# A gated linear attention with an MLP behind it on one core: the first unit is given an order of its own

## The chip, the cores and the metric

The kernel runs on one core of one Trainium2 chip. A core has five engines with a queue of instructions each: TensorE (PE, matrix products, with its weight loads shown as PEld), VectorE (DVE), ScalarE (ACT), GpSimd (POOL) and SyncE (SP, which here only issues DMAs). The engines run side by side and wait for one another through semaphores. Products are written to PSUM, a small memory that the program divides into banks; everything else lies in SBUF. The metric is the time of one execution on the device in microseconds (us).

## The reference, cut to what matters

```python
batch, n_heads, seq, head_dim = (4, 8, 768, 48)

f = 1.0 / (1.0 + np.exp(-f_logit))
state = np.zeros((B, H, D, D), dtype=np.float32)
for t in range(S):
    state = f[:, :, t, :, None] * state + np.einsum('bhd,bhe->bhde', k[:, :, t], v[:, :, t])
    y[:, :, t] = np.einsum('bhd,bhde->bhe', q[:, :, t], state)

x = attn_out.transpose(0, 2, 1, 3).reshape(B * S, H * D)       # 3072 x 384
h = x @ w_in                                                   # 384 x 2048
g = h * (1.0 / (1.0 + np.exp(-1.702 * h)))
out = g @ w_out                                                # 2048 x 384
```

All arrays are float32. A state of 48 x 48 for each of 32 heads decays by a gate of its own in each of its 48 rows, takes up one outer product per token and is read by the query. The result, with heads joined, goes through an MLP with a quick gelu.

## The kernel before, in words

**Units.** The 3072 tokens are cut into twelve units of 256 tokens with all eight heads (`NALL` = 12, `U` = 256, L65 and L81). Each unit is done by `attention(n)`, and its output goes to the MLP as `xT`. Units 0 to 2 (`N_FILL` = 3) are done in one way, later ones in another that does not concern us. Within a unit, chunks of 64 tokens are the grain: inside a chunk the products of gates are built up in six levels (`LEV` = 1, 2, 4, ..., 32, `NL` = 6), between chunks a state is carried.

**What one of the first units does.** `load_raw` (L245) fetches the gate logits, q and k (called j = 0, 1, 2) into `raw`. `turn` (L334) transposes them on PE against an identity, two pieces of eight products each, and ACT copies each piece out of PSUM with two instructions; for the gates that copy is the sigmoid, in units 1 and 2 a tanh with POOL's `half_up` behind it. The three calls are `begin_f`, `begin` (for q) and `begin_k`; the last also sets aside `Kc` for level 0. `begin_gates` has POOL multiply the gates up, level by level, into `tot`.

A level (`level(l)`, L520) then does four things. `score` (L409) multiplies `Kc` of the level with the queries, sixteen products on PE, into a PSUM tile `sc` of two banks of which there is one. `promote` (L484) multiplies k and q by the gates of the level on DVE, an instruction for each, in place in `X`; it then lets ACT copy the next `Kc` (`set_aside`, L468). The q promotion follows the scores, as these read the queries. `evacuate` (L437) copies the scores under a mask into `A`: level 0 by a product with the mask, levels 1 to 4 by two `copy_predicated` on DVE, level 5 by four copies on ACT. The next level's scores write the same `sc`, so they wait for that copy.

Behind the levels come `turn_k` (L550), which turns k back through PE, and the part "S": `add` (L506) starts the values `y` from `A` and v, then the chunk products (L604) of `kn` with v go to PSUM and DVE forms the four states `st` from them, alternating a product with the gates (L622) and a sum (L623). Half of v is used in reversed order; `reverse_v` (L302) makes that with a `stream_shuffle` on DVE. The last part, "W", adds the states' share to `y` (L644), ACT copies `y` to `yT` (L656) and SP sends it to `xT`.

**The MLP and the weights.** Weights arrive as raw bits in pairs (`fetch_weights`, L192, three in flight), and each pair is converted by a Prelu on ACT (`begin_pair`, L208) and four DVE operations (L225 to L228), one for each call of `convert`. The products with w_in are L1034, those with w_out L1048.

**The order.** For units 0 to 3 the order in which instructions are emitted is the order of every engine's queue. `parts_of` lists a unit's parts and puts the next unit's `begin_...` between them; `merge` emits them, and between the parts a share of MLP work from `fill` and a number of converts. Unit 0 has no MLP work beside it; a list tells how many converts follow which part:

```python
fill = []
merge(0, fill, 0, steady, deal=(0, 0, 0, 0, 0, 0, 0, 3, 0, 0, 1, 2))
fill += mlp_blocks((0, 0)) + mlp_blocks((0, 1))
merge(1, fill, UNIT // 2 - LAG // 2 - 3 * DM, steady, 12, hold=1)
```

Here 12 stands for pairs' halves: 24 converts within unit 1. `keep_up` (L108) puts products on PE whose results nobody reads. PSUM tiles other than `sc` and `y` come from `bank` (L103), four lanes of one bank in turn.

Of the kernel before, what the change touches and what calls it, by code (L numbers as in the profile page):

```python
# [23 lines left out]
def kernel(  # L24
# [33 lines left out]
    nc = tc.nc  # L58
# [42 lines left out]
    turns = count()  # L101

    def bank(shape, name, lane=None):  # L103

        lane = next(turns) % 4 if lane is None else lane
        return ps.tile(shape, F32, tag=f"mm{lane}", name=name, bufs=1)
# [207 lines left out]
    def attention(n):  # L314
# [19 lines left out]
        def turn(j, outs, fn=None):  # L334
# [12 lines left out]
            for j0 in range(0, R, 4):  # L347
# [14 lines left out]
            if fn and n:  # L362
                half_up()
# [9 lines left out]
        def begin_f():  # L373
            def decay():
                turn(0, lambda f: F[:, ORDER.index(f) * SLOT:(ORDER.index(f) + 1) * SLOT], sigmoid)
# [5 lines left out]
            if n >= N_FILL or (n == 1 and 0 == 0):  # L381
                load_raw(n + 1, 0)
# [26 lines left out]
        def score(s, l, rhs):  # L409

            for a in range(NP):
                for h, g in TILES:
                    x = (a * NG + g) * HS
                    nc.tensor.matmul(  # L414
                        t["sc"][g * HS:(g + 1) * HS, h, a, s, :], lhsT=t["Kc", l][rows(h), x:x + HS], rhs=rhs(h, a, g),
# [17 lines left out]
        def scores():  # L433
            t["sc"] = ps.tile([P, 2, NP, 2, HS], F32, tag="sc", name=f"sc_{n}_{next(serial)}")
            return t["sc"]

        def evacuate(*levels):  # L437


            for s, l in enumerate(levels):  # L440
                m = LEV[l]
                if m == 1:
                    nc.vector.tensor_tensor(  # L443
                        view(A, 0, [[HALF, 2 * NP], [HS + 1, 2], [2, 32]]),
                        t["sc"].rearrange("p h a s (f t) -> p (h a) s f t", f=2)[:, :, s],
                        masks[:, l].unsqueeze(1).broadcast_to((P, 2 * NP, 2, 32)), ALU.mult,
                    )
                    continue
                if m == 32:

                    for p in range(0, P, 32):
                        f = 1 - p // 32 % 2
                        nc.scalar.copy(
                            view(A[p:p + 32], f * (HS + m), [[HALF, 2 * NP], [1, m]]),
                            t["sc"].rearrange("p h a s t -> p (h a) s t")[p:p + 32, :, s, f * m:(f + 1) * m],
                        )
                    continue
                for at, f in ((HS + m, 1), (0, 0)):
                    dims = [[HALF, 2 * NP], [2 * m, 32 // m], [1, m]]
# [823 lines left out]
```

## Time and profile before

| what | value |
|---|---|
| time, median of 3 runs (lowest to highest) | 609.05 us (609.04 to 609.99) |
| the profiled execution: its own time | 609.42 us |
| its span | 607.6 us |
| mean granted clock of PE | 0.992 |
| PE busy | 580.7 us (96%) |
| DVE busy | 435.0 us (72%) |
| ACT busy | 292.1 us (48%) |
| POOL busy | 139.6 us (23%) |
| chain that ended last | PE 70%, DVE 14%, ACT 6%, issue 4% |

The span is what the trace covers; the time also has what lies around it, 1.8 us in the profiled execution. All positions in the text (such as 14.65) are us from the span's start. The page cuts the span into 40 slices of 15.2 us and gives an engine's busy share of each in tenths; PEclk is the clock that PE was granted, in tenths of full speed. In the timeline a line has start, duration, engine, line of the program, operation, output <- inputs with shapes, the number of instructions, and in brackets the idle time before it with what ended that. The trace counts the products of the scores, turns and other float32 products twice: 32 for the sixteen of a level. "issue" is time in which an engine waited for nothing that the profile shows; SPq and ACTq are the DMA issues of these two engines.

### The profile page before, as it was taken

What the parts mean: (1) busy time and instruction counts of PE and PEld (TensorE: products, weight loads), DVE (VectorE), ACT (ScalarE), POOL (GpSimd) and SP (SyncE); (2) the same over time, 40 slices, a digit from 0 to 9 for tenths busy, and PEclk for the clock granted to TensorE, in tenths of its full rate; (3) what the DMA queues carried; (4) which work ended last, traced back from release to release, by engine and by line L of the source; (5) the groups of instructions that cost most, each with busy time, mean ns of one, the idle gap of its engine ahead of it and who ended that gap; (6) DMA issues with size and microseconds to landing.
All of it is one profiled execution on the core that took longest, in us unless ns stands there. A gap on an engine that the chain in (4) does not pass through costs nothing.

```text
span 607.6 us, 18486 instructions
## 1 busy us (share of the span) xinstructions
PE 580.7 (96%) x7824; PEld 516.5 (85%) x7824; DVE 435.0 (72%) x693; ACT 292.1 (48%) x611; POOL 139.6 (23%) x215
## 2 busy tenths in 40 slices
PE   6769899979999999999999999999999999999897
PEld 5657676847677689999999999999999999999897
DVE  1788976575894967788867888868778686462284
ACT  4475644433332444456465474575474563552440
POOL 3020020050032423240522312502502502303000
PEclk9988999989999999999999999999999999999999
DMA  6847766652034245245443243443352111001000
GB/s 173 209 107 187 176 163 172 140 140 79 1 96 101 77 126 130 50 114 132 92 127 90 68 129 97 118 125 69 93 143 63 55 54 30 27 3 26 28 1 27
DMA packets 83315, 58.30 MB, mean 96 GB/s; under 512 B 33633, under 2 KB 75265, under 8 KB 83233
## 3 DMA queue, kind: packets, MB, share of 16 engines
q1 hardware_dynamic: 82480, 55.94, 36.8%
q10 hardware_dynamic: 753, 1.18, 0.7%
q8 instruction: 62, 1.02, 0.7%
q14 instruction: 20, 0.16, 0.1%
HBM read 43.98 MB, written 8.39 MB: 86 GB/s over the span
## 4 chain that ended last, share of the span: by engine, by line
PE 70%; DVE 14%; ACT 6%; issue 4%; SPq 2%; POOL 2%; DMA 2%; DVEq 0%; ACTq 0%; POOLq 0%
PE h L940 15%; PE h L1034 10%; PE o_Y L803 9%; PE o L1048 7%; PE o_Z L803 6%; PE h_y L940 6%; PE sc L414 5%; PE o_W L803 3%; PE o_X L803 3%; PE t L352 2%; ACT yT L656 2%; POOL tot L405 2%; DVE g L968 1%; PE sc L604 1%; PE y L513 1%
## 5 line engine op out<-in xcount | busy, mean ns | idle before, releaser
L1034 PE MATMUL h<-xT,w_in 128*128 128x256 f32 x384 | 90.2, 390 | 1.2 <-DVE sum L1100 0.6
L473 ACT COPY Kc<-X 128x512 f32<-128x512 f32 x72 | 48.3, 671 | 81.4 <-DVE X L502 57.2
L1034 PEld LDWEIGHTS h<-xT,w_in 128*128 128x128 f32 x384 | 73.2, 194 | 14.0 <-DVE sum L1100 1.2
L502 DVE TENSOR_TENSOR X<-X,tot 128x1024 f32<-128x1024 f32 x45 | 57.4, 1275 | 33.9 <-PE sc L414 23.6
L1048 PE MATMUL o<-w_out,g 128*128 128x384 f32 x192 | 67.7, 502 | 2.7 <-DVE w_out L228 2.3
L1048 PEld LDWEIGHTS o<-w_out,g 128*128 128x128 f32 x192 | 36.2, 194 | 26.2 <-DVE w_out L228 2.9
L405 POOL TENSOR_TENSOR tot<-F 128x512 f32<-128x512 f32 x12 | 12.5, 1041 | 195.9 <-DVE st L622 189.6
L940 PE MATMUL h<-E,w_in 128*128 128x128 f32 (+1 forms) x420 | 53.4, 275 | 0.0
L803 PE MATMUL o_Y<-T,S 128*128 128x192 f32 x288 | 50.6, 329 | 0.0
L940 PEld LDWEIGHTS h<-E,w_in 128*128 128x128 f32 x420 | 50.1, 192 | 0.0
L1038 ACT ACTIVATE g<-h 128x256 f32<-128x256 f32 x64 | 24.0, 383 | 51.9 <-PE h L1034 51.5
L970 ACT ACTIVATE g<-g 128x512 f32<-128x512 f32 (+1 forms) x63 | 35.6, 585 | 25.6 <-DVE g L968 25.0
L803 PEld LDWEIGHTS o_Y<-T,S 128*128 128x128 f32 x288 | 46.8, 190 | 0.5
L656 ACT COPY yT<-y 48x256 f32<-48x256 f32 x96 | 35.2, 367 | 21.0 <-PE y L644 19.9
L464 DVE COPY_PREDICATED A<-masks,sc 128x256 f32<-128x256 uint32 x96 | 42.2, 509 | 0.0
L968 DVE TENSOR_TENSOR g<-g,h 128x512 f32<-128x512 f32 (+1 forms) x52 | 31.8, 632 | 12.7 <-PE h L940 11.5
L367 POOL TENSOR_SCALAR F<-F 128x1024 f32<-128x1024 f32 x11 | 15.1, 1369 | 112.0 <-ACT F L370 89.6
L414 PE MATMUL sc<-X,Kc 48*64 48x64 f32 x1440 | 31.1, 222 | 9.5 <-DVE A L443 3.5
L414 PEld LDWEIGHTS sc<-X,Kc 48*64 48x64 f32 x1440 | 26.3, 136 | 16.2 <-issue 8.3
L340 DVE STREAM_TRANSPOSE X<-raw 128x512 f32<-128x512 f32 x36 | 38.2, 1110 | 0.2
L902 POOL TENSOR_TENSOR E<-xT 128x128 f32<-128x128 f32 (+1 forms) x32 | 20.2, 643 | 75.3 <-DMA xT<-yT 34.7
L968 DVE TENSOR_TENSOR g<-g,h_y 128x512 f32<-128x512 f32 (+1 forms) x26 | 16.5, 633 | 21.8 <-PE h_y L940 18.3
(153 smaller groups left out, 1178.2 us busy)
## 6 DMA issues: line engine op xcount, KB each, us to landing
bits<-in_moe_w_out_dram SPq DMA_DIRECT2D x8, 768.0 KB, 5.5
raw<-in_f_logit_dram SPq DMA_DIRECT2D x48, 96.0 KB, 2.5
raw<-in_k_dram SPq DMA_DIRECT2D x48, 96.0 KB, 3.1
raw<-in_q_dram SPq DMA_DIRECT2D x44, 96.0 KB, 2.3
bits<-in_moe_w_in_dram SPq DMA_DIRECT2D x7, 576.0 KB, 5.2
k_tok<-z SPq DMA_DIRECT2D x56, 64.0 KB, 1.7
kt<-k_tok SPq DMA_DIRECT2D x14, 256.0 KB, 3.0
xT<-yT SPq DMA_DIRECT2D x24, 144.0 KB, 2.6
```

Of the source, the lines that this page charges most:

```text
L340: nc.vector.transpose(view(out, at, [[HALF, NP], [step, R4], [R4 * step, 32]]), by_half[:, j, f].rearrange("p a (j d) -> p (a j) d", j=R4) ...
L414: nc.tensor.matmul(t["sc"][g * HS:(g + 1) * HS, h, a, s, :], lhsT=t["Kc", l][rows(h), x:x + HS], rhs=rhs(h, a, g), start=True, stop=True,)
L464: moved = nc.vector.copy_predicated(out=view(A, at, dims), mask=mask.bitcast(U32), data=got)
L473: nc.scalar.copy(c.rearrange("p (n two m) -> p n two m", two=2, m=m), view(X, KF * SLOT, [[2 * m, SLOT // (2 * m)], [(KR - KF) * SLOT + m, ...
L502: nc.vector.tensor_tensor(x, x, y, ALU.mult)
L656: nc.scalar.copy(view(yT[rows(h)], at, [[U, NP], [step, HS]]), py[columns(h, g), g, :, f, :])
L803: nc.tensor.matmul(t[name], lhsT=lhs(f), rhs=rhs(f), start=(new and i == 0), stop=(i == HF - 1), skip_group_check=True,)
L940: nc.tensor.matmul(ph[:, t], lhsT=WA[a][:, f * P:(f + 1) * P], rhs=E[n][b], start=(root and t == 0), stop=not goes_on, skip_group_check=True,)
L968: nc.vector.tensor_tensor(to, to, part, ALU.add if sign > 0 else ALU.subtract)
L970: nc.scalar.activation(to, to, AF.Gelu_apprx_sigmoid)
L1034: nc.tensor.matmul(ph, lhsT=w_in[:, c, ff * P:(ff + 1) * P], rhs=xTs[n][:, c, :], start=(c == 0), stop=(c == NK - 1))
L1048: nc.tensor.matmul(t["po"], lhsT=g[ff // FG][:, ff % FG, tt * P:(tt + 1) * P], rhs=w_out[:, ff, :], start=(ff == ffs[0]), stop=(ff == ffs[ ...
```

## The change

The first unit leaves `merge` and gets a function of its own, `opening`, which emits its work in another order; later units keep theirs.

- The first weight pair is fetched by SP instead of ACT, behind f and k of unit 0. k is turned ahead of q; `begin_gates` comes ahead of both; the dummy products between the turns go.
- The loads of unit 1's k come ahead of v's, q's behind v's.
- Scores of levels 0 and 1 go to lanes 0 and 1 (`lane_scores`), of levels 2 and 3 to the tile `y`, of levels 4 and 5 to `sc`. `open_level` does scores and promotion only.
- Unit 1's f is turned in two halves, behind levels 2 and 3. One dummy product follows levels 0, 1 and 4, where two followed each of the levels 0 to 2 before.
- The masked copies (`open_evacuate`; here named `evacuate`) follow all levels, in the order 0, 5, 1, 2, shuffle of v, 3, 4. For levels 0 and 1 the tile is in two lanes, so that each copy is two instructions.
- The gelu's table is loaded by a gelu of four numbers ahead of `turn_k`.
- The chunk products come ahead of the values, into lanes 0 and 1; k of unit 1 is turned between them. A copy of one number of `y` onto itself stands on ACT behind the values.
- Four converts follow the states; 26 instead of 24 fall into unit 1.

```diff
     def bank(shape, name, lane=None):
-        lane = next(turns) % 4 if lane is None else lane
+        if lane is None:
+            lane = chosen.pop(0) if chosen else next(turns) % 4
         return ps.tile(shape, F32, tag=f"mm{lane}", name=name, bufs=1)
...
+        def lane_scores(*two):
+            t["sc"] = [bank([P, NP, 2, HS], f"sc_{n}_{next(serial)}", lane) for lane in two]
+            t["both"] = [(h * NP, x.rearrange("p a s t -> p a s t")) for h, x in enumerate(t["sc"])]
...
+        def open_level(l):
+            if l % 2 == 0:
+                lane_scores(0, 1) if l == 0 else scores("y" if l == 2 else "sc")
+            by_level[l] = t["both"]
+            score(l % 2, l, queries(l))
+            promote(l)
+
+        def open_evacuate(l):
+            for c, sc in by_level[l]:
+                evacuate_one(l, c, sc[:, :, l % 2])
...
         @part("S")
         def _():
-            add()
-            pd = scores().rearrange("p h a s t -> p h (a s t)")
+            if n:
+                add()
+                pd = scores().rearrange("p h a s t -> p h (a s t)")
+                pd = [pd[:, g] for g in range(NG)]
+            else:
+                pd = [bank([P, NP * 2 * D], f"pd_{g}", g) for g in range(NG)]
...
+            if not n:
+                units[1][0][2]()
+                add()
+
+                seen = t["py"][HS:HS + 1, 1, 0, 1, :1]
+                nc.scalar.copy(seen, seen)
             load_v(n + 1)
...
-    load_raw(0, 1, (nc.scalar,))
-    fetch_weights(nc.scalar)
-    begin_f, *begin = units[0][0]
-    begin_f()
-    keep_up(2)
-    for fn in begin:
-        fn()
-    load_raw(1, 0)
-    load_v(0)
-    load_raw(1, 1)
-    load_raw(1, 2)
-    fetch_weights()
-    fetch_weights()
+    def opening():
+        begin_f, begin, begin_k, begin_gates = units[0][0]
+        next_f, next_q, next_k, next_gates = units[1][0]
+        level, evacuate, turn_k = units[0][2]
+        load_raw(0, 0)
+        load_raw(0, 2)
+        load_raw(0, 1, (nc.scalar,))
+        fetch_weights()
+        begin_f()
+        begin_gates()
+        begin_k()
+        begin()
+        load_raw(1, 0)
+        load_raw(1, 2)
+        load_v(0)
+        load_raw(1, 1)
+        fetch_weights()
+        fetch_weights()
+        for l in range(NL):
+            chosen[:] = [2, 3][l % 2:][:1]
+            level(l)
+            if l in (2, 3):
+                next_f((0, 4)[l - 2:][:1])
+            elif l < NL - 1:
+                keep_up(1)
+            if l == 1:
+                begin_pair(0)
+                state["begin"] = 1
+
+        nc.scalar.activation(q_end, q_end, AF.Gelu_apprx_sigmoid)
+        chosen[:] = [2, 3]
+        turn_k(0)
+        turn_k(2)
+        evacuate(0)
+        evacuate(NL - 1)
+        for l in range(1, NL - 1):
+            evacuate(l)
+            if l == 2:
+                units[0][3]()
+        chosen[:] = [2, 3, 2, 3]
+        next_q()
+        units[0][1][-2][1]()
+        next_gates()
+        for _ in range(NOP):
+            convert()
+
     fill = []
-    merge(0, fill, 0, steady, deal=(0, 0, 0, 0, 0, 0, 0, 3, 0, 0, 1, 2))
+    opening()
     fill += mlp_blocks((0, 0)) + mlp_blocks((0, 1))
-    merge(1, fill, UNIT // 2 - LAG // 2 - 3 * DM, steady, 12, hold=1)
+    merge(1, fill, UNIT // 2 - LAG // 2 - 3 * DM, steady, 13, hold=1)
```

## The prediction

> **What bounds the kernel now.** I read the page's forty slices first, then the chain of waits, then the timeline of the first 85 us, where the change is.
>
> ```profile
> PE   6769899979999999999999999999999999999897
> DVE  1788976575894967788867888868778686462284
> PEclk9988999989999999999999999999999999999999
> ```
>
> The slices show PE at 90% or more from about 135 us to near the end; only the first slices have room. A change to the first unit must therefore hand an earlier start to a PE-bound remainder. In the opening three things hold PE back.
>
> ```profile
> 5.95 2.31 ACTq L205 DMA_DIRECT2D bits<-in_moe_w_in_dram  x2
> ...
> 8.31 1.21 ACT L357 ACTIVATE F<-t 128x256 f32<-128x256 f32 x4 [6.08 <-PE t L352]
> ...
> 19.67 0.69 PE L414 MATMUL sc<-X,Kc 48*64 48x64 f32 x32 [0.82 <-DVE A L464]
> 20.43 0.69 DVE L498 TENSOR_TENSOR X<-X,tot 128x512 f32<-128x512 f32 x1 [0.38 <-PE sc L414]
> 21.04 0.75 DVE L464 COPY_PREDICATED A<-masks,sc 128x256 f32<-128x256 uint32 x2
> 21.93 0.69 PE L414 MATMUL sc<-X,Kc 48*64 48x64 f32 x32 [0.29 <-DVE A L464]
> ...
> 29.14 0.69 PE L414 MATMUL sc<-X,Kc 48*64 48x64 f32 x29 [1.84 <-issue]
> ...
> 33.00 1.21 PE sc L604 x60
> ```
>
> (The last line is from the chain of waits, the others from the timeline.) First, ACT issues weight DMAs until 8.26 and so begins the sigmoid late. Second, a level's scores wait for the masked copy (L464) of the level before, because they share one PSUM buffer. Third, the states' products (L604) stand behind the values (L513) and the last copies.
>
> ```profile
> 34.43 0.35 DVE L619 COPY st<-sc 128x192 f32<-128x192 f32 x1
> ...
> 37.12 1.70 DVE L228 TENSOR_TENSOR w_in<-a,s 128x768 f32<-128x768 f32 x1
> ...
> 38.92 0.78 DVE L225 TENSOR_SCALAR s<-a 128x768 int32<-128x768 int32 x1
> ...
> 40.30 1.42 DVE L498 TENSOR_TENSOR X<-X,F 128x512 f32<-128x512 f32 x2
> ...
> 42.47 1.13 PE L414 MATMUL sc<-X,Kc 48*64 48x64 f32 x32 [3.29 <-DVE A L443]
> ...
> 43.85 5.23 PE L1034 MATMUL h<-xT,w_in 128*128 128x256 f32 x12 [0.25 <-DMA xT<-yT]
> ...
> 51.67 0.69 DVE L498 TENSOR_TENSOR X<-X,tot 128x512 f32<-128x512 f32 x1 [1.52 <-PE sc L414]
> ```
>
> This is the hand-over to unit 1, whose first promotion starts at 40.30. PE idles 3.29 us and comes back slow: 12 h products take 5.23 us, against 2.86 at 51.53. The clock by windows:
>
> ```profile
> 28.00:30.00 2.00, 0.86 (x31) 0.79 (x32) 0.13 (x1) 0.13 (x1) 0.00 (x0) 1.00 0.69 136
> ...
> 42.00:44.00 2.00, 1.28 (x33) 1.12 (x33) 1.97 (x3) 0.60 (x1) 0.00 (x0) 0.50 0.43 98
> ...
> 48.00:50.00 2.00, 2.00 (x22) 1.52 (x22) 1.97 (x3) 0.38 (x1) 0.00 (x0) 0.83 0.99 211
> 60.00:80.00 20.00, 17.86 (x364) 13.40 (x363) 19.09 (x32) 14.26 (x31) 4.67 (x6) 1.00 0.69 161
> 80.00:100.00 20.00, 20.00 (x168) 14.80 (x167) 13.47 (x25) 7.21 (x15) 0.07 (x1) 1.00 0.63 150
> ```
>
> After the window come the busy times of PE, PEld, DVE, ACT and POOL, the granted clock, the DMA share and GB/s. The clock is 0.50 until about 48.6. From 60 to 80 us DVE is full (19.09 of 20), from 80 to 100 PE is.
>
> **The change, part by part.** I follow the new instruction order with the old durations.
>
> *Start.* The 2.31 us of weight DMAs leave ACT's queue, and k is turned before q. The first sixteen f matmuls are half of 3.44 us (done at 6.4), the rest at 8.10; F is complete near 8.9 instead of 9.52. Without four dummies (8.04 to 9.31) k's turn follows at 8.11 and q's behind it, four pieces of 0.93 (64 in 3.71 us), done at 9.04, 9.97, 10.90, 11.83. ACT copies each piece in 0.66, with Kc 0 (0.84) between k and q: done 12.95. First scores at 13.0 instead of 14.65: 1.65 earlier. Weights now stand on SP ahead of the next f, at most 2.31 us, but that f waits for PE until 8.14 anyway. Unknown: whether q, used at 9.97, lands later beside weights issued 1 us sooner. Zero to 1 us; I take zero, as PE took q at 9.38 without a wait.
>
> *Levels.* With three bank pairs the wait on the copy goes. The next wait is the q promotion: scores to its start 0.76 (19.67 to 20.43), itself 0.69, then about 0.17 to the next scores: 1.62 a level, against 2.26 (19.67 to 21.93). The other path, k promotion (0.68), Kc copy (0.62) and two hops, is shorter. The Prelu put into ACT's order (0.93) and F's copies (0.66 each) fit beside it; unit 1's f pieces take 0.95 of PE's 0.92 gap. Its weights, issued by 7.2, land by 14.7 (longest row 7.5 us); the Prelu comes at 15.7. POOL's tot, now ending near 12.1, can stretch the first k promotion by 0.74 (L228 took 1.70 beside it and 0.96 alone); hidden, as the q promotion comes only at 13.8. Sixth scores: 13.0 + 5 x 1.62 = 21.1; last promotion ends at 22.55, before at 30.56. That includes the 1.84 us PE stall at 27.30, whose cause the trace doesn't show. I take it as gone from the path: the same number of PE instructions is now reached in q's turn for unit 1, where PE has slack. If it returns on the path, +1.84.
>
> *Copies behind.* Nothing hides them: DVE does level 0 (0.68), 1 (1.09 to the next start), 2 (0.68), the shuffle (0.49), 3 and 4 (0.68 each), 4.3 us, plus 0.2 for the split instructions and a short hop: shuffle done at 25.8, all at 27.15. v's second half lands by 21.1 (SP issued it until 15.44, now 1.79 later with k ahead of it, longest row of v 3.9), so 4 us of cover before the shuffle. Unit 1's q, behind both, lands at 23.1 by the longest row (issue until 17.33 + 1.79, then 4.0); its turn comes at 23 and PE has 1 us to spare before the states' products. ACT's gelu table load (1.28, was at 45.50) and four level 5 copies (1.51) end at 25.1.
>
> *States ahead.* Products need the shuffle: PE 25.95 to 27.15 (1.21), hiding behind the last copies. Seven state operations took 2.69 (34.43 to 37.12): done at 30.0, so 7.1 earlier. On PE the k turn (1.97) and values (1.11) end at 30.2; ACT's new 1x1 copy lies between zero and 0.20 (the 128x1 ACTIVATE at 2.02) plus two hops of 0.15; I take 0.5. State products 30.75 to 31.85, eight yT copies (3.02) to 34.97. Before, yT ended at 40.61 and h began 3.24 later: h now at 38.2, 5.65 earlier.
>
> *Hand-over.* Before, w_in, s and a took 3.18 us from 37.12 to 40.30. Now four converts stand there: 0.78 + 0.64 + 0.96 + 1.70 beside POOL's tot = 4.08. Unit 1's first promotion at about 34.15, 6.15 earlier; but two converts of pair 1 (1.4) are no longer done, so **4.75** of DVE work gained. (6 + 24 converts become 4 + 26: the later two fall into DVE's full stretch.) Later on SP, q_end's two DMAs (0.43 each) move ahead of weights; hidden, since SP waited 6.1 us there for DVE.
>
> *Clock.* sc_8 and its dummy end at 33.4; the next scores need the promotion and copy, 34.15 + 2.14 = 36.3. PE idles 2.9 us. Idle of 1.84 us (28 to 30) left the clock at 1.00; idle of 2.33 did not:
>
> ```profile
> 126.59 5.19 PE L1048 MATMUL o<-w_out,g 128*128 128x384 f32 x10 [2.33 <-DVE w_out L228]
> ...
> 128.00:129.00 1.00, 1.00 (x3) 0.59 (x2) 1.00 (x2) 0.00 (x0) 1.00 (x1) 0.50 1.02 390
> ```
>
> So I take half clock again, as before: h takes its 5.23, the scores at 50.91 come 5.65 earlier, q promotion at 46.0. One convert of 0.56 to 0.96 is outstanding there: 4.9, agreeing with 4.75. If the gap came out under 1.84 and the clock stayed, h would take 2.86, scores would come at 42.9, and DVE would set the pace: 34.15 + 9.17 (40.30 to 49.47) + 1.16 - 0.96 for the regrouped converts + 0.68 = 44.2, which is 1.8 more.
>
> The Trainium skill, page "TensorE: Matmul & The Clock Gate", section "Part 1: The HAM clock gate (the "warmup" mystery)", puts the fall to half rate after at least one idle window of about 3.4 us. By that rule 2.9 us idle would keep the clock and the gain would be 6.6, an estimate; the row with 2.33 us idle and a clock of 0.50 contradicts it.
>
> *Downstream.* The chain of waits from 51.7 to 75 is nearly all DVE, after 79.6 mostly PE, and DMA falls to a share of 0.00 at 150 to 160: nothing runs to a fixed clock. Bounds: none or all of the lead arrives. I take all.
>
> **Sum.** 4.8 off the profiled execution's 609.42 (span 607.6 and 1.8 around it) is 604.6. The median of three runs is 0.37 lower: **604.3**.
>
> **Rivals.**
> *Levels don't shorten.* If the Kc copy or promotion keeps the period at 2.26, 5 x 0.64 = 3.2 goes back: 607.5. For: ACT is in order and now holds Prelu and turns. Against: Kc 4 was ready at 23.09 and its scores waited for t pieces, not for it.
> *The lead is swallowed.* Later waits keep their places: 609, within 0.2%. For: PE also idles at 124 to 126 behind DVE. Against: those DVE operations are themselves relative.
> *Slower: the opening goes cold.* Four groups of dummies of 1.34 us become three of about 0.67. If PE falls to half clock at the 1.1 us gap before 13.0 and stays there, six scores cost 0.43 more each (1.13 against 0.70): 2.6; turns 1.5 for 32 (3.44 against 1.97), twice: 3.0; the products' 64-matmul groups of 1.1 about double, three times: 3.3. Less 4.8 that is +4: 613. It decides when more than half of that is met. Against: idle of 1.63 (13.02 to 14.65) and 1.84 kept the clock.
>
> **Chances and range.** Likeliest, 0.58 (its own range 601.8 to 606). Levels or the PE stall taking back part, 0.16. Swallowed, 0.09. Slower by cold clock or late loads, 0.17. Low end: 4.8 + 1.8 + 1.1 for two later DVE waits (0.84 at 54.6, 0.31 at 59.2) that an earlier PE would spare: 601.4, rounded to 601.5. High: the stall 1.84, q 1.0 and most of the levels' case: 608. 0.2% (1.2 us) is what measurement can tell: faster 0.74, same 0.09, slower 0.17.
>
> **What would show it.** First scores near 13.0; score spacing near 1.6 with no wait for a masked copy; states done near 30; unit 1's first promotion near 34; h at 38; the granted clock 0.50 after 36; PE solid from 75. Wrong if scores wait for ACT, if the clock is 0.50 before 30, or if SP's loads for unit 1 land after 23.

## The result: no change that can be measured

The changed kernel takes 609.51 us (median of 12 executions, 608.47 to 612.0), the kernel before 609.04 us (12 executions, 608.64 to 611.69): a ratio of 1.0003, 95% interval 0.9988 to 1.0017. (The ratios here and below are those on record with their intervals; they are not quotients of two medians.) The forecast of 604.3 was wrong. The profiled execution of the changed kernel took 609.87 us, with a span of 608.0 (before: 609.42 and 607.6) and a mean granted clock of 0.986 (before: 0.992).

From the page of the changed kernel, busy tenths in 40 slices of 15.2 us:

```profile
PE   7869899969999999999999999999999999999897
DVE  2797976565894867788867888868778686462284
PEclk9979999979999999999999999999999999999999
```

PE has gained in the second slice, as it should. But PEclk now shows a 7 in the third and in the ninth slice (30 to 46 and 122 to 137 us).

The timeline of the changed kernel, with the lines that answer to those shown of before (start, duration, engine, line, operation; in brackets the idle time and what ended it):

```profile
16.15 0.70 PE L416 MATMUL sc<-X,Kc 48*64 48x64 f32 x32 [0.16 <-DVE X L510]
...
21.05 0.69 PE L416 MATMUL sc<-X,Kc 48*64 48x64 f32 x32 [0.17 <-DVE X L510]
...
24.11 1.50 ACT L466 COPY A<-sc 32x256 f32<-32x256 f32 x4
...
25.26 1.98 DVE L476 COPY_PREDICATED A<-masks,sc 128x128 f32<-128x128 uint32 x6 [1.64 <-ACT A L466]
...
27.79 1.38 PE L634 MATMUL pd<-vt,kn 64*64 64x48 f32 x56 [0.76 <-DVE vt L306]
29.10 3.21 PE L354 MATMUL t<-ident,raw 128*64 128x128 f32 x32
...
29.20 0.36 DVE L655 COPY st<-pd 128x192 f32<-128x192 f32 x1 [0.15 <-PE pd L634]
...
34.11 1.04 PE L680 MATMUL y<-X,st 48*48 48x64 f32 x46 [0.75 <-ACT y L645]
...
36.12 1.35 DVE L510 TENSOR_TENSOR X<-X,F 128x512 f32<-128x512 f32 x2
...
39.11 1.13 PE L416 MATMUL sc<-X,Kc 48*64 48x64 f32 x32 [2.70 <-ACT Kc L485]
...
41.87 4.56 PE L1070 MATMUL h<-xT,w_in 128*128 128x256 f32 x12 [1.62 <-DMA xT<-yT]
```

The levels do what the change says: scores come every 1.6 us and no longer wait for a masked copy; the sixth set starts at 21.05 instead of 29.14. Behind them the lead melts. VectorE waits 1.64 us for ScalarE's level-5 copies before it can copy level 1. The k turn at 29.10 takes 3.21 us instead of 1.97, at half clock. The first h starts at 41.87 and not at 38.2.

The chain of waits of the changed kernel around the first h (start, duration, what):

```profile
38.00 0.36 ACT yT L692
38.38 0.46 ACT Kc L485
38.85 2.98 DMA xT<-yT
41.83 0.04 issue
41.87 4.56 PE h L1070 x12
```

The windows of the changed kernel (busy time of PE, PEld, DVE, ACT, POOL, then the granted clock, the DMA share and GB/s):

```profile
28.00:30.00 2.00, 2.00 (x64) 1.91 (x58) 1.74 (x6) 0.00 (x0) 0.00 (x0) 0.57 0.21 36
42.00:44.00 2.00, 2.00 (x5) 1.63 (x6) 1.88 (x3) 0.24 (x1) 0.00 (x0) 0.50 0.78 202
...
132.00:134.00 2.00, 2.00 (x85) 2.00 (x81) 0.10 (x1) 0.69 (x2) 0.00 (x0) 0.50 0.00 0
```

Half clock stands at 28.3 to 31.7, 38.5 to 45.4 and 130.7 to 137.5; before it stood at 41.9 to 48.7 and 127.2 to 130.6. The third place decided this execution. Before, PE's wait of 2.33 at 126.59 (shown in the prediction) was followed by slow o products, and they only filled time in which PE would have waited for unit 3's promotion anyway. The two kernels on PE there, before and then after:

```profile
132.79 1.11 PE L644 MATMUL y<-X,st 48*48 48x64 f32 x64 [1.02 <-DVE X L502]
...
134.78 1.56 PE L1048 MATMUL o<-w_out,g 128*128 128x384 f32 x4
```

```profile
125.02 3.49 PE L1084 MATMUL o<-w_out,g 128*128 128x384 f32 x10 [2.94 <-DVE w_out L230]
131.22 1.96 PE L680 MATMUL y<-X,st 48*48 48x64 f32 x64 [2.71 <-DVE X L514]
...
134.81 7.39 PE L1084 MATMUL o<-w_out,g 128*128 128x384 f32 x18
```

After, the o products ran at full clock (3.49), PE then waited 2.71 for the promotion, and the clock fell behind that wait, under work that nothing hides: y 1.96 instead of 1.11, eighteen o products 7.39 instead of 6.07. The y state started 1.57 earlier than before (131.22 against 132.79); the o products behind it, at 134.81, were level.

Three positions account for every profile of this study: unit 1's level-2 scores, unit 2's y state, and the end.

| kernel | first h | unit 1 level-2 scores | unit 2 y state | span | median us | ratio to before (95%) |
|---|---|---|---|---|---|---|
| before | 43.85 | 50.91 | 132.79 | 607.6 | 609.04 | 1 |
| after | 41.87 | 48.26 | 131.22 | 608.0 | 609.51 | 1.0003 (0.9988-1.0017) |
| e1 level 5 last | 42.37 | 49.24 | 132.45 | 607.5 | 608.93 | 0.9988 (0.9975-1.0002) |
| e2 unit 2 filled, banks shifted | 42.52 | 49.54 | 132.73 | 610.4 | 612.43 | 1.0055 (1.0032-1.0078) |
| e3 the same on before | 44.25 | 51.78 | 133.67 | 608.4 | 610.88 | 1.0025 (1.0013-1.0037) |
| e4 start delayed | 43.99 | 50.60 | 133.55 | 610.4 | 612.23 | 1.0050 (1.0030-1.0070) |
| e5 after, unit 2 filled | 42.01 | 48.31 | 131.28 | 606.0 | 608.58 | 0.9992 (0.9980-1.0003) |
| e6 before, unit 2 filled | 44.62 | 51.51 | 133.51 | 608.4 | 609.17 | 0.9996 (0.9986-1.0006) |
| e7 copies reordered | 42.47 | 49.92 | 132.88 | 607.6 | 608.37 | 0.9985 (0.9970-1.0000) |
| e8 = e7, unit 2 filled | 41.04 | 47.44 | 130.42 | 605.2 | 607.41 | 0.9972 (0.9961-0.9983) |
| e9 = e8, load later | 40.01 | 48.04 | 131.02 | 606.1 | 607.03 | 0.9953 (0.9938-0.9968) |
| e10 = e8, opening filled | 43.05 | 49.35 | 132.29 | 607.0 | 606.69 | 0.9952 (0.9934-0.9970) |
| e11 = e8, both | 42.89 | 47.58 | 130.56 | 605.6 | 604.99 | 0.9934 (0.9909-0.9959) |
| e12 = e6, opening filled | 43.68 | 48.37 | 132.53 | 607.6 | 608.87 | 0.9990 (0.9978-1.0002) |
| e13 = e5, opening filled | 41.84 | 48.11 | 131.07 | 605.8 | 609.04 | 0.9993 (0.9975-1.0011) |
| e14 = e13, load later | 41.68 | 46.34 | 129.34 | 604.4 | 606.85 | 0.9964 (0.9950-0.9977) |
| e15 = e12, load later | 43.66 | 48.34 | 132.02 | 607.1 | 609.06 | 1.0001 (0.9987-1.0015) |

From the y state to the end of the span every profile has 474.7 to 475.1 us, but for the three in which half clock lies over the work behind that state (after 476.8, e4 476.9, and e2 477.7, which also waits for a bank there). So what is gained or lost lies ahead of 131 us or in that one fall. One profile is one execution, and positions of the same program scatter by some 3 us (the last experiments show how); medians and intervals carry the sizes, profiles the mechanisms.

### The profile page after: what moved, and what is told of

It is laid out like the page before. It is cut to its first block, busy times and chain, and to the rows that moved or that the text cites. A ratio compares the mean times of both kernels' runs of the same rounds, so it can differ in the third digit from the quotient of the medians.

```text
span 608.0 us, 18479 instructions
## 1 busy us (share of the span) xinstructions
PE 579.3 (95%) x7814; PEld 517.4 (85%) x7814; DVE 436.0 (72%) x696; ACT 291.4 (48%) x613; POOL 139.2 (23%) x215
## 4 chain that ended last, share of the span: by engine, by line
PE 71%; DVE 12%; ACT 6%; DMA 4%; issue 3%; POOL 2%; SPq 2%; DVEq 0%; ACTq 0%; POOLq 0%
PE h L976 14%; PE h L1070 10%; PE o_Y L839 9%; PE o L1084 8%; PE o_Z L839 6%; PE sc L416 6%; PE h_y L976 5%; PE o_X L839 3%; PE o_W L839 3%; PE t L354 2%; ACT yT L692 2%; POOL tot L407 2%; PE y L680 1%; DVE g L1004 1%; DVE X L342 1%
## 5 line engine op out<-in xcount | busy, mean ns | idle before, releaser
L1006 ACT ACTIVATE g<-g 128x512 f32<-128x512 f32 (+1 forms) x63 | 35.5, 582 | 25.8 <-DVE g L1004 25.4
L692 ACT COPY yT<-y 48x256 f32<-48x256 f32 x96 | 35.1, 366 | 22.3 <-PE y L680 21.1
L476 DVE COPY_PREDICATED A<-masks,sc 128x256 f32<-128x256 uint32 (+1 forms) x98 | 42.1, 503 | 1.7 <-ACT A L466 1.6
L1004 DVE TENSOR_TENSOR g<-g,h 128x512 f32<-128x512 f32 (+1 forms) x52 | 31.7, 631 | 12.5 <-PE h L976 11.5
L938 POOL TENSOR_TENSOR E<-xT 128x128 f32<-128x128 f32 (+1 forms) x32 | 17.7, 562 | 74.4 <-DMA xT<-yT 33.0
L1004 DVE TENSOR_TENSOR g<-g,h_y 128x512 f32<-128x512 f32 (+1 forms) x26 | 16.5, 633 | 22.0 <-PE h_y L976 21.1
```

What stands on the lines that cost most here:

```text
L476: moved = nc.vector.copy_predicated(out=view(A, c * HALF + at, dims), mask=mask.bitcast(U32), data=got)
L692: nc.scalar.copy(view(yT[rows(h)], at, [[U, NP], [step, HS]]), py[columns(h, g), g, :, f, :])
L1004: nc.vector.tensor_tensor(to, to, part, ALU.add if sign > 0 else ALU.subtract)
L1006: nc.scalar.activation(to, to, AF.Gelu_apprx_sigmoid)
```

## The experiments

"Theory A": the lead shrinks inside the opening, through waits and TensorE's clock, and what is left is lost to the clock behind unit 2. "Theory B": something downstream (VectorE, a transfer) keeps its time whatever the opening does. "Filled" means matmuls on PE that feed nothing, put into its waits to hold the clock.

**e1, ScalarE's level-5 copies last.**

```diff
         evacuate(0)
-        evacuate(NL - 1)
         for l in range(1, NL - 1):
...
         next_q()
+        evacuate(NL - 1)
```

> The changed kernel, but ACT's four copies of level 5 stand behind DVE's copies of levels 0 to 4 and behind unit 1's q turn, instead of between levels 0 and 1. If the opening's loss against the forecast came from DVE waiting for them (1.64 us before the copies of level 1), the shuffle comes near 26.1 instead of 27.17, the states' products near 26.3 in one piece, the states are done near 30.5 instead of 32.0 and unit 1's first promotion starts near 34.5 instead of 36.12. If that wait only stood in for another, the promotion stays at 36. On the time: if leads reach the end, 1.5 us less than the changed kernel, near 608; if what comes near 130 us swallows them, no difference.

608.93 us. In VectorE's timeline the wait is gone:

```profile
23.43 0.74 DVE L457 TENSOR_TENSOR A<-sc,masks 128x256 f32<-128x256 f32 x2
24.09 1.89 DVE L476 COPY_PREDICATED A<-masks,sc 128x128 f32<-128x128 uint32 x6
25.90 0.01 DVE L306 LOAD_MASK_SELECT vt<-vr  x1
```

The states end at 30.52 (32.04 in the changed kernel, 30.0 forecast). So this wait was real. The first h still comes at 42.37, but this profile does not tell whether something else would have held it: PE stalled 1.99 us in the values, yT ended only at 38.00 (38.36 in the changed kernel), and SP took 1.75 us over one of xT's issues.

**e2 and e3, the wait ahead of unit 2's y state filled in the changed kernel, the o products' wait in the kernel before.**

```diff
+                if n == N_FILL:
+                    keep_up(3)
                 rest = ahead()
```

```diff
+            if (n, tt, ff) == (0, 0, 10):
+                keep_up(3)
             if ff == ffs[0]:
```

> The changed kernel with three dummy products (about 2.0 us) on PE between the last output products of unit 2's part and its state products, where PE idled 2.71 us (128.5 to 131.2) and then ran at a granted clock of 0.50 until 137.5. If the lead of 1.57 us is lost to that clock, the clock stays at 1.00, the state products take 1.1 instead of 1.96, the next eighteen output products 6.1 instead of 7.39, and the time falls by 1.5 to 2 us, to about 607.7. If DVE or unit 3's loads set the pace there, PE only waits later and the time stays at 609.5.

> The kernel before with three dummy products in its own gap in the same stretch (124.26 to 126.59), after which its clock was 0.50 from 127.1 to 130.6. There PE still waited 1.02 us for DVE behind the slow products, so if the clock theory holds a warm clock is worth nothing there: between 609.0 and 609.4, and it may get worse (to 610.5) if PE then idles 2.7 us ahead of the state products and goes cold there, as the changed kernel does. If a cold clock costs its full 1.8 us wherever it falls, 607.3.

612.43 and 610.88 us, both slower. The added matmuls took a bank from the turn of four and shifted all later ones by one. In e2's timeline of PE the y state is warm, but an h group behind it meets a bank that VectorE has not yet read:

```profile
132.73 1.11 PE L680 MATMUL y<-X,st 48*48 48x64 f32 x64
...
142.70 7.57 PE L1070 MATMUL h<-xT,w_in 128*128 128x256 f32 x26 [1.92 <-DVE sum L1136]
```

These two settle nothing on the clock; e5 and e6 repeat them with the turn of the banks unchanged.

**e4, the first scores delayed by four matmuls that feed nothing.**

```diff
         fetch_weights()
         fetch_weights()
+        chosen[:] = [3]
+        keep_up(4)
         for l in range(NL):
```

> The changed kernel with four dummy products ahead of the first scores, which come about 1.7 us later (14.6 instead of 12.87); everything of unit 0 follows. If a shift in unit 0 reaches the end, 611.2. If the stretch near 130 us swallows shifts, 609.5 again. If the time goes with where the clock's fall happens, anything between 608.5 and 611.5, with the positions of the low clock in the profile telling which.

612.23 us, 2.7 more than the changed kernel. In the profiles the first scores are 2.35 later (15.22), unit 2's y state 2.33, the span 2.4. A delay in the opening is passed on in full, so nothing downstream has slack to hide one. That does not yet show that a lead arrives too; e5, e8 and e14 do, where y states at 131.28, 130.42 and 129.34 are followed by spans that end at 606.0, 605.2 and 604.4. With them Theory B falls.

**e5 and e6, unit 2's waits filled in both kernels, banks unchanged.** (e6 has three in the first wait.)

```diff
+            if (n, tt, ff) == (0, 0, 10):
+                chosen[:] = [next(copy(turns)) % 4]
+                keep_up(4)
...
+                if n == N_FILL:
+                    chosen[:] = [next(copy(turns)) % 4]
+                    keep_up(3)
```

> The changed kernel with seven small matmuls added on TensorE that feed nothing, in the two waits of unit 2's end: four in the wait ahead of the ff loop's eleventh o-product group (about 122 to 125 us) and three in the wait ahead of unit 2's state products (about 128.5 to 131). They take the output banks that the next of the kernel's own would take, so the turn of the banks is unchanged. Theory A (the lead of 1.57 us that stands at 117 us is lost because TensorE falls to half clock from 130.7 to 137.5): the granted clock stays at 1.00 through this stretch, the y state takes about 1.1 instead of 1.96 and the eighteen o groups about 6.1 instead of 7.39, the lead stays, and the time is 1.5 to 2 us below the changed kernel's, 607.5 to 608. Theory B (something other than TensorE's clock holds the later work to the old times): the clock stays, the y state is early, and the time is again 609.0 to 609.8.

> The kernel before with the same small matmuls in the same two waits (three and three, its first wait being shorter), the turn of the banks unchanged. Theory A: in the kernel before, the half clock of 127.2 to 130.6 lay beside a wait that it used up, so a full clock there gives little: 608.5 to 609.5. Against the changed kernel with the same matmuls it shows what the change's lead is worth once the clock is alike: 1.0 to 2.0 us by theory A, 0 by theory B.

608.58 and 609.17 us. PE's timeline of e5:

```profile
125.07 3.49 PE L1088 MATMUL o<-w_out,g 128*128 128x384 f32 x10 [0.79 <-DVE w_out L231]
128.40 1.78 PE L117 MATMUL idle<-masks,ident 128*128 128x320 f32 x6
131.28 1.11 PE L681 MATMUL y<-X,st 48*48 48x64 f32 x64 [1.11 <-DVE X L515]
...
133.27 6.07 PE L1088 MATMUL o<-w_out,g 128*128 128x384 f32 x18
```

The y state stands where it stood in the changed kernel (131.28), the clock stays whole behind it, and the span ends 2.0 us sooner at 606.0. That is the lost lead, in one execution. Over the medians e5 is 0.9 below the changed kernel and 0.6 below e6, and its interval still holds 1. The fall behind unit 2 costs what the profile says when it happens; it does not happen each time (e18).

**e7 and e8, the copies in another order, and the same with unit 2's waits filled.**

```diff
-                seen = t["py"][HS:HS + 1, 1, 0, 1, :1]
-                nc.scalar.copy(seen, seen)
...
+            if not n:
+                seen = t["py"][HS:HS + 1, 1, 0, 1, :1]
+                nc.vector.tensor_copy(seen, seen)
...
-        evacuate(0)
-        evacuate(NL - 1)
-        for l in range(1, NL - 1):
+        units[0][3]()
+        for l in range(NL - 1):
             evacuate(l)
-            if l == 2:
-                units[0][3]()
...
         next_q()
+        evacuate(NL - 1)
```

> The changed kernel with its first unit's copies put in another order: the shuffle ahead of all masked copies on VectorE, then levels 0 to 4, then unit 1's q turn, with ScalarE's four level-5 copies last, and the 1x1 copy that orders the values ahead of the state products on VectorE behind the states instead of on ScalarE behind k's copies. Theory A (the forecast 4.8 fell to 1.6 inside the opening because of ScalarE's copies standing between level 0 and level 1, the half clock of 28.3 to 31.7 that followed, and the 1x1 copy behind ScalarE's other work): no wait of VectorE on ScalarE between levels 0 and 1, the products of the states in one piece near 26, no TensorE gap of 2 us at 25.8 to 27.8, the first h near 39 to 40 instead of 41.87, unit 1's level-2 scores near 46 to 47 instead of 48.26; the time 1 to 3 us below the changed kernel's, 606.5 to 608.5. Theory B: the opening becomes shorter by as much, but the time stays at 609 to 609.8.

> The reordered first unit together with the seven small matmuls in unit 2's waits. Theory A: both gains add, the time is 3 to 4.5 us below the changed kernel's, 605 to 606.5. Theory B: 609 to 609.8. If the reordered unit alone gains as much as both together, the clock of unit 2 is not what costs the lead.

608.37 and 607.41 us; the second falls short of the 605 to 606.5 expected. In VectorE's timeline of e7 shuffle and copies run without a wait (24.08 to 28.44), PE does the states' products in one piece, and no half clock follows at 28. yT ends at 37.40 and 36.29 (38.36 in the changed kernel). The first h, expected at 39 to 40, comes at 42.47 and 41.04. Here a new question opened: h came 3.2 us after yT's end in the kernel before, and 5.1 and 4.75 after it here.

**e9 to e12, the load ahead of xT, and the opening's waits.** SP issues 768 KB of w_out as soon as VectorE's third convert of the first pair has read its bits (between 33.8 and 37.8 us), and the transfers from yT to xT directly behind it. e9 puts the load behind them; e10 fills PE's two waits ahead of the first h; e11 does both; e12 fills the wait of the kernel before (`keep_up(6)` at the first place, nothing at the second).

```diff
             state["done"] += 2
-            fetch_weights()
+            if state["fetch"] != 3:
+                fetch_weights()
...
             half(1)
+            if not n:
+                fetch_weights()
```

```diff
-                parts[0] = kind, lambda: (head(), load_raw(n + 1, 1), keep_up(1))
+                parts[0] = kind, lambda: (head(), load_raw(n + 1, 1), keep_up(1 if n != 1 else 4))
...
+                if (n, ff) == (0, 0):
+                    chosen[:] = [next(copy(turns)) % 4]
+                    keep_up(3)
                 t["ph"] = bank([P, U], f"h_{n}_{ff}")
```

> The reordered kernel with the matmuls in unit 2's waits, and one load moved: the 768 KB of w_out that SP issued just ahead of the transfers that turn yT into xT (at 34.5 us) is issued just behind them. Until now the first h started 3.2 us after yT's end in the kernel before, where that load had landed by then, and 4.75 to 5.1 us after it in the versions that end yT at 36.3 to 37.4. Theory A (xT's transfers wait behind this load's packets, so that the first h cannot come before about 41 however early yT is): the first h starts at 39.2 to 39.8 instead of 41.04, and the time is 0.5 to 1.5 us below the 607.41 of the kernel with the load ahead. Theory B (xT's transfers take their 5 us by themselves, or are late for another reason): h stays at 41, and the time is 607.0 to 608.0.

> The reordered kernel with the matmuls in unit 2's waits, and six more matmuls that feed nothing in TensorE's two waits ahead of the first h (34.8 to 37.6 and 38.7 to 41.0). Theory A (unit 1's pace is set by TensorE here, at the half clock of 37.5 to 44.3): the clock stays at 1.00, the first twelve h matmuls take 2.9 us instead of 4.57, unit 1's level-2 scores start near 45.6 instead of 47.44, and the time is 1 to 2 us below 607.41. Rival (VectorE's conversions and promotions, busy without a gap from 32 to 46, set the pace): the clock stays and h is short, but the level-2 scores come at 47 and the time is 607.0 to 608.0.

> The load behind xT's transfers and the matmuls in the opening's waits together (four of them, since the wait for xT should be shorter). Theory A for both: the first h near 39.5, short, unit 1's level-2 scores near 44.3, the time 604.5 to 606.5. If only one of the two binds, the time of that one alone. If VectorE sets unit 1's pace, 607.0 to 608.0.

> The kernel before with the matmuls in unit 2's waits and five more in its wait of 3.3 us ahead of the first h. Theory A: the clock of 41.9 to 48.7 stays at 1.00, the first twelve h matmuls take 2.9 instead of about 5 us, the time is 1 to 2 us below the 609.17 without these five, 607.2 to 608.2; what then stands between this kernel and the reordered one with a warm opening is the worth of the shorter first unit when the clock is alike, 1.5 to 3 us. Rival (VectorE sets unit 1's pace): 608.7 to 609.7.

607.03, 606.69, 604.99 and 608.87 us. SP's and PE's timelines of e8, then of e9:

```profile
34.51 0.38 SPq L208 DMA_DIRECT2D bits<-in_moe_w_out_dram  x1
...
41.04 4.57 PE L1072 MATMUL h<-xT,w_in 128*128 128x256 f32 x12 [2.32 <-DMA xT<-yT]
```

```profile
38.85 0.53 SPq L208 DMA_DIRECT2D bits<-in_moe_w_out_dram  x1
...
40.01 1.22 PE L1075 MATMUL h<-xT,w_in 128*128 128x256 f32 x2 [1.46 <-DMA xT<-yT]
...
41.50 4.64 PE L1075 MATMUL h<-xT,w_in 128*128 128x256 f32 x10 [0.26 <-DMA xT<-yT]
```

In e9 yT ends at 36.47 and h starts at 40.01, 3.5 later. But only its first two products do: the other ten waited for the rest of xT until 41.50, so that h ended later than in e8 (46.14 against 45.61). In this profile moving the load alone brings h's start forward and not its end, and the intervals of e8 and e9 overlap. In e10 filling was not enough: PE still waited 2.49 us for xT, the clock fell at 44.2 to 47.6, and in this execution the level-2 scores came late (49.35). e11 (with one matmul in the second place) is the best version, in six executions, by 0.41 to 0.91% against the kernel before. Its profiled execution was the second slowest of its six (607.42) and had lost clock at 34.4 to 41.3 behind a PE stall of 2.34 us that the profile calls "issue"; so the profile understates it, and the two executions at a mean clock of 1.0 took 603.83 and 605.23.

e12 is the control: with the clock whole (mean 0.997 to 1.0 in all eleven) the kernel before stays at 608.87. Its twelve h products take 2.86 and its level-2 scores come 2.5 earlier, at 48.37, but unit 2's y state comes at 132.53 against 132.79. The 2.5 us are given back between 48 and 85 us, where VectorE's timeline shows no wait up to 84.8 (33.91 of 36 us busy from 48 to 84), and in this kernel the clock in the opening is worth next to nothing. So filling alone does not explain e11's gain.

**e13 to e15, the change as made with all waits filled, with the load behind, and the load behind in the kernel before.** The edits are those above (six matmuls in the first wait, two or one in the second).

> The change as it was made (its own order of copies, the load of w_out ahead of xT's transfers), with the matmuls that feed nothing in unit 2's waits and seven more in its two waits ahead of the first h (35.6 to 39.1 and 40.3 to 41.9). The half clock of 28 to 32 is left as it is. Against the kernel before with its waits filled in the same way (608.87) it shows what the change as made is worth when TensorE keeps its clock from 35 us on; against the reordered kernel with a warm opening (606.69) what the order of the copies adds. Theory 1 (the clock took most of the lead): 606.5 to 607.3, no more than 0.5 us above the reordered one. Theory 2 (the order of ScalarE's and VectorE's copies and the late 1x1 copy took most of it): 607.7 to 608.6, within 1.2 us of the kernel before.

> The same with the 768 KB load of w_out behind xT's transfers. yT ends near 37 to 38.4 in the change as made, only 1 to 3 us after the load's issue, so that less is to be had than in the reordered kernel (where the load's place was worth 0.4 to 1.7 us): the first h at 40.3 to 41.5 instead of 41.9, the time 0.2 to 1 us below the same kernel with the load ahead. If the load's place is worth nothing here, the two are alike within 0.3 us.

> The kernel before with its waits filled and the 768 KB load of w_out behind xT's transfers. There the load (issued at 34.6) had landed before xT's transfers began (39.1), so theory A expects no gain from its place: 608.6 to 609.5, the first h at 43.5 to 44. If this kernel becomes faster too, by more than 0.5 us, the load's place is worth something by itself and its gain in the reordered kernel is not the change's.

609.04, 606.85 and 609.06 us. The load's place is worth 2.2 us of the medians in the change as made (the two intervals overlap by a hair, and e14 has one matmul less in the second place) and nothing in the kernel before. SP's timeline, then PE's, of e13:

```profile
34.98 0.39 SPq L208 DMA_DIRECT2D bits<-in_moe_w_out_dram  x1
35.46 0.61 SPq L724 DMA_DIRECT2D xT<-yT  x1
...
38.01 1.22 SPq L729 DMA_DIRECT2D xT<-yT  x2
...
38.55 1.34 PE L117 MATMUL idle<-masks,ident 128*128 128x320 f32 x4
41.84 4.44 PE L1074 MATMUL h<-xT,w_in 128*128 128x256 f32 x12 [1.95 <-DMA xT<-yT]
```

and of e14:

```profile
37.02 0.61 SPq L727 DMA_DIRECT2D xT<-yT  x1
...
39.57 1.22 SPq L732 DMA_DIRECT2D xT<-yT  x2
40.89 0.53 SPq L208 DMA_DIRECT2D bits<-in_moe_w_out_dram  x1
...
41.68 2.83 PE L1077 MATMUL h<-xT,w_in 128*128 128x256 f32 x12 [0.95 <-PE idle L117]
46.34 0.69 PE L418 MATMUL sc<-X,Kc 48*64 48x64 f32 x32
```

In e13 the last issue for xT ends at 39.23 and h waits until 41.84; that wait drops the clock from 41.7 to 45.1, in spite of the filling, and h takes 4.44. So e13 did not keep the clock that its expectation supposed, and its two theories cannot be told apart by it; what it shows is that yT 1.65 earlier than in the changed kernel's profile (36.71 against 38.36), with the same order of copies, left h where it was. In e14 this execution's yT is even later (38.51 against 36.71, through a half clock at 28.9), yet h starts sooner, at full clock, and the level-2 scores come 1.77 sooner. The forecast position was 45.3.

Laid side by side, with the load ahead, the first h follows the load's issue by 6.5 to 7.1 us in ten profiles (after, e2, e4, e5, e7, e8, e13, e16 to e18), while its distance from yT's end goes from 3.3 to 5.4; e10 (8.0) and e1 (8.6, where SP took 1.75 us over one of xT's issues) are later still. With the load behind xT, or long landed as in the kernel before, h follows yT's end by 3.1 to 3.5 (before, e9's first two products, e12, e14, e15); in e11 it stood behind the filling.

**e16 to e18, more profiled executions: two of e13's kernel, one of the changed kernel.**

> A second profiled execution of the change with its waits filled (the kernel of e13). Of the twelve executions timed there, four took 606.3 to 607.7 and eight 609.0 to 610.6, at the same mean clock of 0.997, and only one of the four is profiled. If this one falls among the eight: by theory A its two us more lie ahead of unit 1's level-2 scores (48.11 in the profile at hand, near 50 here), with the rest of the span alike within 0.3 us (557.7 from these scores to the end); by a rival they lie behind unit 2's y state, where no profile has shown any difference at full clock.

> A third profiled execution of the same kernel, to see one of the slower eight with more certainty; the same expectations.

> A second profiled execution of the changed kernel as it is. Theory A: whenever the clock falls between 125 and 140 us behind a wait of more than 2 us, the time from unit 2's y state to the end is near 476.8 instead of 474.8; whenever it falls beside the wait itself (as in the kernel before) it is near 474.8, and the lead of the opening is kept (607 to 608).

609.12, 610.95 and 609.32 us. From the level-2 scores to the end e13, e16 and e17 have 557.7 us each; those scores start at 48.11, 49.49 and 51.29. In these three the scatter is made in the opening. e17 shows how, on PE:

```profile
15.16 1.44 PE L117 MATMUL idle<-masks,ident 128*128 128x320 f32 x2
16.53 1.13 PE L417 MATMUL sc<-X,Kc 48*64 48x64 f32 x32
17.59 1.97 PE L355 MATMUL t<-ident,raw 128*64 128x128 f32 x16
```

Half clock from 15.1 to 22.0, behind the gaps of the first two levels: the forecast's rival of a cold opening, met in one execution of three. e16 differs from e13 in the moment at which the clock first rises (10.3 against 7.6); its first scores come at 13.91 instead of 12.81. In e18 the y state, which had stood at 131.22 in the first profile of this kernel, came at 132.71, the clock fell at 126.0 to 129.4 beside the wait, and 474.7 us followed:

```profile
126.50 4.91 PE L1084 MATMUL o<-w_out,g 128*128 128x384 f32 x10 [2.94 <-DVE w_out L230]
132.71 1.11 PE L680 MATMUL y<-X,st 48*48 48x64 f32 x64 [1.30 <-DVE X L514]
...
134.69 6.07 PE L1084 MATMUL o<-w_out,g 128*128 128x384 f32 x18
```

So the two profiles of the changed kernel end nearly alike (608.0 and 607.4) for two reasons: an early opening that lost 2.0 behind unit 2, and an opening 1.5 later that lost nothing there.

## Why the prediction was wrong, step by step

- *Start*: right. First scores at 12.87 (13.0).
- *Levels*: right. Period 1.6 (1.62), sixth scores at 21.05 (21.1); the PE stall of 1.84 did not come back on this path.
- *Copies behind*: wrong by the term that was not there. The shuffle ended at 27.7, not 25.8: level 1's copy waited 1.64 us for the four level-5 copies, which the order of emission puts ahead of it on the same tile. The forecast had these copies end at 25.1 and put VectorE's wait for them at nothing; this is the first step that failed. e1 and e7 remove the wait.
- *States ahead*: states ended at 32.04 (30.0), by the same wait. The k turn took 3.21 instead of 1.97, as the products in three pieces left PE idle for 1.40 us and the clock fell at 28.3. That was in part bad luck: the same 1.40 us kept the clock in e5. "The clock is 0.50 before 30" was one of the forecast's own signs of being wrong. State products at 34.11 (30.75), yT at 38.36 (34.97): of these 3.4 us some 1.8 are the late shuffle, 1.4 the half clock and 0.2 the 1x1 copy.
- *The first h at yT's end plus 3.24*: in the changed kernel's profile this measured 3.51, so that h (41.87 for 38.2) was late there almost wholly because yT was. But an earlier yT would not have brought the forecast's h. The 3.24 was read in a profile where w_out's 768 KB were issued 4.5 us ahead of xT's first transfer; in the changed kernel it is 1.6, for the load comes when the third convert frees its buffer (34.58 before, 35.28 after) while yT moved toward it. h then keeps to the load: yT earlier by 1.4 to 1.65 (e5, e13) left h at 42.0 and 41.84. That xT's transfers wait behind the load's is inferred from such positions and from e13 to e15; no run shows it packet by packet. An estimate of what this step alone cost: with the states at 30.0 and the converts as forecast, the load would be issued at 32.5, and 6.5 to 7.1 behind it h comes at 39.0 to 39.6, 0.8 to 1.4 later than forecast.
- *Hand-over*: four converts took 4.16 (4.08). The first promotion came at 36.12 (34.15), late by the *Copies behind* wait. Between the level-2 scores and the y state the changed kernel takes 1.08 more (82.96 against 81.88). The two converts that unit 1 has more of were forecast at 1.4 and would account for it, but no run took them away.
- *Clock*: the fall at 38.5 came as forecast, and h took 4.56 (5.23 was priced). Not priced were a new fall at 28 and one behind unit 2: this term, put at nothing, cost 2.0 us in the first profile. Nor does the length of a wait decide, as the forecast took it from 1.84 and 2.33 us: 1.40 us lost the clock at 28.3, and 2.94 us ending at 125.02 kept it (last section).
- *Downstream*: the premise, nothing runs to a fixed clock, is right (e4, e14). "All of the lead arrives" is not: of 5.65 us forecast at unit 1's level-2 scores 2.65 were there (1.14 in e18), 1.57 remained at unit 2's y state, and in the first profile the last was lost to the clock. So the 5.2 us by which that span missed the forecast (0.4 more than before instead of 4.8 less) are 3.0 up to those scores, 0.2 between them and the y state, and 2.0 in the clock behind it.
- *Rivals*: "swallowed, 609" had the time by luck and not by its mechanism, for the later waits did move. "Goes cold" is a part of the scatter.

In the recorded ratios: with its waits filled the change as made stands where the kernel before stands (0.9993); with the load behind xT it is 0.36% faster, with the copies reordered as well 0.66%, 4.0 us, near the 4.8 forecast, though that is another kernel than the one forecast. The same edits without the change give 0.9990 and 1.0001. How much of the difference between e13 and e11 is the copies' order alone is not settled: e11 against e14 differ by 1.9 us in medians, with intervals that overlap. The load behind xT without any filling wasn't tried, nor was a kernel without the 1x1 copy, whose values and state products would write one bank without an order.

## What to carry to other kernels

A latency taken from a trace (here 3.24 us from yT to h) holds for the traffic that stood beside it there; when a change moves its start, look for the load that is issued just ahead on the same queue and for what triggers that load. Where an engine copies into a tile that another engine also writes, the order of emission is a wait, so put the engine that is free later last. When a change shortens one side of a wait, the wait grows on the other side, and with a clock that falls behind idle time the price may be paid in the work after it, a hundred microseconds on.

## What the runs showed of the hardware

The granted clock moves on a grid. Behind its first rise, every low stretch up to the last products in the twenty profiles is one, two, three or four times 3.41 us long, and the grid's position differs from one execution to the next (the first full clock comes between 7.6 and 10.7 us). The Trainium skill, page "TensorE: Matmul & The Clock Gate", section "Part 1: The HAM clock gate (the "warmup" mystery)", says this of the window: free-running, 3413 ns. Its rule that half rate follows at least one idle window the runs do not bear out, if idle means a whole window. Cutting each profile's first 180 us into windows from its first full clock, and adding up PE's idle time in each window at full clock: with 1.8 us or more the next window was at half clock in 24 of 24, with less than 1.2 in none, and in between (31 windows) in 7. Where the idle time falls matters as much as how long it is: in the changed kernel the wait of 2.94 us ending at 125.02 lay 1.77 and 1.16 in two windows and kept the clock, the wait of 2.33 in the kernel before lay within one and lost it.

PE also stalled for 0.3 to 2.3 us in the values of the reordered versions and of e1 (1.99 in e1, 2.34 in e11) with nothing in the profile that it waited for; the cause stays open.
